# Logits of the next chunk computed in one run with the tap sums of this one, with the VectorE, GpSimd and SyncE work moved to suit

## The chip, the cores and the metric

One NeuronCore of one Trainium2 chip runs the whole kernel. The metric is device time in microseconds of one execution; lower is better. A kernel's figure is the median of its runs. The profile is one execution taken by the hardware profiler.

## The reference, cut to what matters

The input x is 2048 x 512 in bf16, layer-normalized to xn. Two branches start from xn: a local attention with 32 heads of 16, in which each position looks at 8 earlier ones at a distance of 2, and a gated feed-forward of width 1792.

```python
xn = layernorm(x)
q, k, v = split(xn @ wqkv)                      # 32 heads of 16
logits[s, w] = q[s] . k[s - 2 * w] / 4          # w = 0..7, positions below 0 masked
o[s] = sum_w softmax(logits)[s, w] * v[s - 2 * w]
s = o @ wo
g = silu((gelu(xn @ w_gate) * (xn @ w_up)) @ w_down)
out = x + s * g
```

## The kernel before

The positions are cut into four chunks of 512 (j = 0..3; the prediction calls them "tiles 0 to 3" where it speaks of the attention, and "tiles 8 to 11" are the blocks of 128 positions of chunk 2). For each chunk TensorE does a gate/up stage (14 pairs of projections), then q, k, v of the next chunk, then the down projection in four groups, with the output projection between them. The attention lies beside it: VectorE multiplies q by shifted k (`pk`), TensorE sums over the head with a matrix of ones that is only 32 columns wide (the logits), ScalarE takes exp, VectorE multiplies by shifted v (`pv`), and TensorE sums again (the tap sums and the denominators). These sums use a quarter of the array's columns each; four of them, writing to different partitions, run side by side (in the trace their starts lie 3 to 4 ns apart).

```python
def logits(j):                                  # 32 matmuls with 32 columns each
    nc.scalar.preload_act_table(AF.Exp)
    L = att.tile([P, NC, TQ], F32, name="L_ps", tag="quad")
    for wh in range(WH):
        for c in range(NC):
            for wl in range(WL):
                nc.tensor.matmul(L[H * wl : H * (wl + 1), wh, :], lhsT=dsum[:, c, :],
                                 rhs=st[j]["pk"][WL * wh + wl][:, c, :], ...)
    nc.scalar.activation(out=E[:], in_=L[:, 0:WH, :], func=AF.Exp, scale=SCALE)

# ... the places in the schedule, for j = 1..3
for w in range(W):
    at(("qkv", j, 9 + w) if w < 3 else ("down", j - 1, w // 3), qk_product, j, w)
at(("glu", j, 0), logits, j)                    # a run of 32-column matmuls
for i in range(8):
    at(("glu", j, 2 + i), av_product, j, i // 2, i % 2)
at(("glu", j, 11), denominators, j)             # a second run, with
at(("glu", j, 11), av_sums, j)                  # 8 + 32 such matmuls
```

`at(key, f, ...)` puts f into the program just ahead of the stage named by the key. All engines run their programs in order.

The softmax here doesn't subtract the row's maximum and nothing guards it: scores larger than these inputs give would overflow.

## Time and profile before

| | before |
|---|---|
| median of 6 runs | 229.99 us (229.64 to 230.21) |
| span of the profiled run | 228.0 us, granted clock 1.000 |
| TensorE busy | 222.4 us, 98% |
| VectorE, ScalarE busy | 147.6 us, 129.8 us |
| runs of 32-column matmuls | 8 |
| first logits matmul to start of the last matmul | 190.25 us |

The lines are in the prediction. In a trace, matmul records can be missing; then two neighbours seem 0.432 us apart and not 0.216. Weight loads are all recorded.

### The profile page before, as it was taken

The numbers are of one execution on the slowest core, as the hardware profiler recorded it, in microseconds if no ns is written. First come the engines' busy times: TensorE is split into PE (matmuls) and PEld (weight loads), VectorE is DVE, ScalarE is ACT, GpSimd is POOL, SyncE is SP. The second block draws the span as 40 slices with busy tenths as digits, with TensorE's granted clock in tenths as the row PEclk, the third lists the DMA queues.
The fourth block names the chain that finished last, engine by engine and source line by source line (L and its number), as shares of the span: only waits on it lengthen the run. The fifth ranks groups of instructions, "written<-read, shape, count | busy, mean of one in ns | idle before, by whom it ended". The sixth has DMA issues, their size and how long they took to land.

```text
span 228.0 us, 3495 instructions
## 1 busy us (share of the span) xinstructions
PE 222.4 (98%) x1300; PEld 106.8 (47%) x1320; DVE 147.6 (65%) x234; ACT 129.8 (57%) x213; POOL 12.8 (6%) x44
## 2 busy tenths in 40 slices
PE   8999999999999999999999999999999999999993
PEld 6864444444444444444444444444444444444453
DVE  4585996999496298865945369735476429943324
ACT  3779769774423876467621686746642387647210
POOL 1046023100000000110000000000000000000000
PEclk9999999999999999999999999999999999999999
DMA  6999589971399211110287511110149700001011
GB/s 166 354 372 372 146 169 197 247 202 38 101 195 206 70 25 29 26 29 0 92 169 168 139 30 23 26 35 5 39 119 206 169 27 3 0 6 26 0 45 48
DMA packets 31264, 24.62 MB, mean 108 GB/s; under 512 B 10896, under 2 KB 31248, under 8 KB 31248
## 3 DMA queue, kind: packets, MB, share of 16 engines
q1 hardware_dynamic: 31248, 24.41, 42.8%
q8 instruction: 10, 0.16, 0.3%
q14 instruction: 6, 0.05, 0.1%
HBM read 18.74 MB, written 4.34 MB: 101 GB/s over the span
## 4 chain that ended last, share of the span: by engine, by line
PE 95%; ACT 2%; issue 1%; DVE 0%; ACTq 0%; DVEq 0%
PE u_ps L238 21%; PE y_ps L394 21%; PE g_ps L238 19%; PE qkv_ps L238 17%; PE s_ps L410 6%; PE L_ps L295 3%; PE o_ps L357 3%; PE warm_ps L220 2%; PE q_ps L238 1%; ACT u L384 1%; ACT L382 1%; PE tr L203 1%; PE den_ps L315 0%; ACT xnT L212 0%; ACT ge L382 0%
## 5 line engine op out<-in xcount | busy, mean ns | idle before, releaser
L238 PE MATMUL u_ps<-xnT,wu_sb 128*128 128x512 bf16 x224 | 57.5, 379 | 0.3
L238 PE MATMUL g_ps<-xnT,wg_sb 128*128 128x512 bf16 x213 | 56.3, 379 | 0.4
L394 PE MATMUL y_ps<-wd_sb,h 128*128 128x512 bf16 (+1 forms) x236 | 50.2, 366 | 0.1
L386 DVE TENSOR_TENSOR h<-ge,u 128x512 bf16<-128x512 bf16 x56 | 23.7, 424 | 37.0 <-ACT u L384 36.6
L284 DVE TENSOR_TENSOR pk<-q_sb,k_sb 128x2048 bf16<-128x2048 bf16 x32 | 37.5, 1216 | 7.0 <-ACT k_sb L259 7.0
L382 ACT ACTIVATE ge<-g_ps 128x512 bf16<-128x512 f32 x56 | 33.5, 598 | 14.9 <-PE g_ps L238 13.8
L384 ACT ACTIVATE u<-u_ps 128x512 bf16<-128x512 f32 x56 | 33.5, 598 | 14.7 <-PE u_ps L238 14.7
L238 PE MATMUL qkv_ps<-xnT,wqkv_sb 128*128 128x512 bf16 (+1 forms) x203 | 40.5, 354 | 0.3
L343 DVE TENSOR_TENSOR pv<-E,v_arr 128x2048 bf16<-128x2048 bf16 x32 | 38.6, 1218 | 0.2 <-issue 0.2
L394 PEld LDWEIGHTS <-h 128*128 128x128 bf16 x238 | 23.3, 98 | 25.3
L238 PEld LDWEIGHTS <-wu_sb 128*128 128x128 bf16 x224 | 21.9, 98 | 26.6 <-issue 0.3
L238 PEld LDWEIGHTS <-wg_sb 128*128 128x128 bf16 x224 | 21.3, 98 | 27.3 <-issue 3.0
L402 ACT ACTIVATE sl<-y_ps 128x512 bf16<-128x512 f32 (+1 forms) x17 | 9.7, 572 | 41.4 <-PE y_ps L394 39.0
L238 PEld LDWEIGHTS <-wqkv_sb 128*128 128x128 bf16 x224 | 21.8, 98 | 19.8 <-issue 0.4
L418 DVE TENSOR_TENSOR m<-s_ps,sl 128x512 bf16<-128x512 f32 (+1 forms) x17 | 11.2, 657 | 22.2 <-PE s_ps L410 22.2
L410 PE MATMUL s_ps<-wo_sb,oT 128*128 128x512 bf16 (+1 forms) x66 | 15.8, 366 | 0.2
L262 ACT ACTIVATE vst<-qkv_ps 128x512 bf16<-128x512 f32 x16 | 9.6, 598 | 6.5 <-PE qkv_ps L238 6.5
L188 POOL TENSOR_TENSOR rstd<-rstd,mhalf 128x1 f32<-128x1 f32 x12 | 7.7, 640 | 87.4 <-DVE rstd L185 87.4
L259 ACT ACTIVATE k_sb<-qkv_ps 128x512 bf16<-128x512 f32 (+1 forms) x20 | 10.2, 516 | 3.5 <-PE qkv_ps L238 3.2
L369 DVE TENSOR_TENSOR oT<-o_ps,rb 128x1024 bf16<-128x1024 f32 x8 | 9.4, 1216 | 3.1 <-DMA rb<-rs_d 3.1
L256 ACT ACTIVATE q_sb<-qkv_ps 128x512 bf16<-128x512 f32 (+1 forms) x16 | 8.7, 544 | 3.2 <-PE qkv_ps L238 3.0
L410 PEld LDWEIGHTS <-oT 128*128 128x128 bf16 x68 | 6.7, 98 | 7.2
(46 smaller groups left out, 105.9 us busy)
## 6 DMA issues: line engine op xcount, KB each, us to landing
v_arr<-vT SPq DMA_DIRECT2D x16, 520.0 KB, 5.4
vT<-vst SPq DMA_DIRECT2D x16, 128.0 KB, 1.8
out_dram<-o_t SPq DMA_DIRECT2D x15, 128.0 KB, 1.8
wg_sb<-in_B_w_gate_dram SPq DMA_DIRECT2D x2, 896.0 KB, 10.7
wu_sb<-in_B_w_up_dram SPq DMA_DIRECT2D x2, 896.0 KB, 12.3
wd_sb<-in_B_w_down_dram SPq DMA_DIRECT2D x1, 1792.0 KB, 12.3
wqkv_sb<-in_A_wqkv_dram SPq DMA_DIRECT2D x3, 512.0 KB, 5.2
x_sb<-in_A_x_dram SPq DMA_DIRECT2D x3, 512.0 KB, 11.6
```

The lines of the kernel that those rows point to most:

```text
L238: nc.tensor.matmul(ps, lhsT=w[:, dk, lo : lo + P], rhs=xnT[j][:, dk, i0 : i0 + n], start=(dk == 0), stop=(dk == NC - 1),)
L259: nc.scalar.activation(out=k_sb[:, c, lo : lo + n], in_=ps, func=AF.Copy)
L262: nc.scalar.activation(out=vst[:], in_=ps, func=AF.Copy)
L284: nc.vector.tensor_tensor(out=pk[:], in0=st[j]["q"][:], in1=k_sb[:, :, off : off + TQ], op=ALU.mult)
L343: nc.vector.tensor_tensor(out=pv[:], in0=st[j]["E"][:, wh, :].unsqueeze(1).to_broadcast([P, 4, TQ]), in1=st[j]["va"][:, 4 * g : 4 * g + 4, ...
L382: nc.scalar.activation(out=ge[:], in_=g_ps[:], func=AF.Gelu_apprx_tanh)
L384: nc.scalar.activation(out=u[:], in_=u_ps[:], func=AF.Copy)
L386: nc.vector.tensor_tensor(out=h[:], in0=ge[:], in1=u[:], op=ALU.mult)
L394: nc.tensor.matmul(y[:], lhsT=st[j][fc][:, tt * P : (tt + 1) * P], rhs=wd_sb[:, fc, cols], start=(fc == 0), stop=(fc == NF - 1),)
L402: nc.scalar.activation(out=sl[:], in_=y[:], func=AF.Silu)
L410: nc.tensor.matmul(s[:], lhsT=st[j]["oT"][:, g, tt * P : (tt + 1) * P], rhs=wo_sb[:, g, cols], start=(g == 0), stop=(g == NC - 1),)
L418: nc.vector.tensor_tensor(out=m[:], in0=s[:], in1=sl[:], op=ALU.mult)
```

## The change

The intent is to enter and leave the 32-column form of the array less often: the logits of chunk j + 1 move into the same run as the denominators and tap sums of chunk j. Everything else serves that. The products for the logits are needed some 12 us earlier, so they are made in halves, and the q and k pieces of a chunk are projected in turns (two of q, two of k, and again) so that the first halves can start early; work of VectorE is moved out of their way; the v read of chunk 0 is moved forward; k gets a tile per chunk (two buffers in turn) and GpSimd copies the 16 columns of overlap; the last four products of chunks 1 to 3 (w = 4 to 7) share v's buffer, so v is read after the logits; the four output projections of a chunk come together at its end.

```diff
+    def sums(j):
+        if j + 1 < NJ:
+            nc.scalar.preload_act_table(AF.Exp)
+        denominators(j)
+        av_sums(j)
+        if j + 1 < NJ:
+            logits(j + 1)
+        reciprocals(j)
+        store_reciprocals(j)
+        spread_reciprocals(j)
+        if j + 1 < NJ:
+            load_v(j + 1)
 ... (for j = 1..3)
-        for w in range(W):
-            at(("qkv", j, 9 + w) if w < 3 else ("down", j - 1, w // 3), qk_product, j, w)
-        at(("glu", j, 0), logits, j)
+        at(("qkv", j, 2), k_halo, j)
+        for i in range(2):
+            at(("qkv", j, 4 + 4 * i), qk_products, j, range(W), 2 * i, 2)
 ... (normalization of chunk 2, from the gate/up stage to the down stage)
-        at(("glu", 0, 7 + i), moments, 2 * TPQ + i)
-        at(("glu", 0, 8 + i), normalize, 2 * TPQ + i)
+        at(("down", 0, 1), moments, 2 * TPQ + i)
+        at(("down", 0, 2), normalize, 2 * TPQ + i)
 ... (v of chunk 0)
-    at(("glu", 0, 0), transpose_by_dma, TPQ + 2)
+    at(("glu", 0, 0), transpose_by_dma, TPQ + 2, (0, 1))
     at(("glu", 0, 0), load_v, 0)
+    at(("glu", 0, 0), transpose_by_dma, TPQ + 2, (2, 3))
 ... (the down stage)
+            for tt in range(TPQ):
+                run("down", j, tt)
+                sl.append(down(j, tt, full))
+                if tt == 0:
+                    sums(j)
+            divide(j)
+            for tt in range(TPQ):
+                finish(j, tt, full, sl[tt])
 ... (longer programs)
+        for _ in range(20):
+            nc.gpsimd.memset(filler[:], 0.0)
+        n = 4 if j < 2 else 2        # pv of chunks 2 and 3 in halves
```

More of the change, by code (lines that the diff above doesn't have):

```diff
@@ L59 @@
     qp = pool("qp", 1)
-    ep = pool("ep", 2)
+    kp = pool("kp", 2)
+    ep = pool("ep", 1)
     vap = pool("vap", 1)
-    prod = pool("prod", 8)
-    hp = pool("hp", 16)
+    prod = pool("prod", 12)
+    hp = pool("hp", 14)
     xtp = pool("xtp", 2)
@@ L66 @@
     sm = pool("sm", 3)
+    slp = pool("slp", 4)
     sm2 = pool("sm2", 2)
@@ L141 @@
     dsum = const.tile([P, NC, H], BF16, name="dsum")
+    filler = const.tile([P, 1], F32, name="filler")
     def sum_constants():
+        for _ in range(20):
+            nc.gpsimd.memset(filler[:], 0.0)
         nc.gpsimd.memset(dsum[:], 0.0)
@@ L155 @@
     xnT = {}
-    k_sb = big.tile([P, NC, PAD + S], BF16, name="k_sb")
-    nc.vector.memset(k_sb[:, :, 0:PAD], 0.0)
+    k_sb = {0: kp.tile([P, NC, PAD + TQ], BF16, name="k_sb")}
+    nc.vector.memset(k_sb[0][:, :, 0:PAD], 0.0)
     stats = const.tile([P, NT, nc.vector.BN_STATS_DIM], F32, name="stats")
@@ L223, in warm_up, with transpose_by_dma @@
             )
-    def transpose_by_dma(t):
+    def transpose_by_dma(t, cs=range(NC)):
         j, i = divmod(t, TPQ)
-        if i == 0:
+        if i == 0 and 0 in cs:
             xnT[j] = xtp.tile([P, NC, TQ], BF16, name="xnT")
-        for c in range(NC):
+        for c in cs:
             nc.sync.dma_start(
@@ L257, in qkv @@
         elif which == 1:
-            lo = PAD + j * TQ + i0
-            nc.scalar.activation(out=k_sb[:, c, lo : lo + n], in_=ps, func=AF.Copy)
+            lo = PAD + i0
+            nc.scalar.activation(out=k_sb[j][:, c, lo : lo + n], in_=ps, func=AF.Copy)
         else:
@@ L268, in load_v @@
         if wls[0] == 0:
-            st[j]["va"] = vap.tile([P, DH, VW], BF16, name="v_arr")
+            st[j]["va"] = vap.tile([P, DH, VW], BF16, name="v_arr", tag="va")
         va = st[j]["va"]
@@ L279, in load_v, with k_halo, qk_products @@
             )
-    def qk_product(j, w):
-        pk = prod.tile([P, NC, TQ], BF16, name="pk", tag="prod")
-        off = PAD + j * TQ - w * DIL
-        nc.vector.tensor_tensor(
-            out=pk[:], in0=st[j]["q"][:], in1=k_sb[:, :, off : off + TQ], op=ALU.mult
-        )
-        st[j]["pk"][w] = pk
-    def logits(j):
-        nc.scalar.preload_act_table(AF.Exp)
-        L = att.tile([P, NC, TQ], F32, name="L_ps", tag="quad")
+    def k_halo(j):
+        k_sb[j] = kp.tile([P, NC, PAD + TQ], BF16, name="k_sb")
+        nc.gpsimd.tensor_copy(out=k_sb[j][:, :, 0:PAD], in_=k_sb[j - 1][:, :, TQ : TQ + PAD])
+    def qk_products(j, ws, c0, n):
+        for w in ws:
+            if w not in st[j]["pk"]:
+                if j and w >= WL:
+                    if w == WL:
+                        st[j]["pk4"] = vap.tile([P, WL, NC, TQ], BF16, name="pk4", tag="va")
+                    st[j]["pk"][w] = st[j]["pk4"][:, w - WL]
+                else:
+                    st[j]["pk"][w] = prod.tile([P, NC, TQ], BF16, name="pk", tag="prod")
+            off = PAD - w * DIL
+            nc.vector.tensor_tensor(
+                out=st[j]["pk"][w][:, c0 : c0 + n, :],
+                in0=st[j]["q"][:, c0 : c0 + n, :],
+                in1=k_sb[j][:, c0 : c0 + n, off : off + TQ],
+                op=ALU.mult,
+            )
+    def logits(j):
+        if j == 0:
+            nc.scalar.preload_act_table(AF.Exp)
+            quad = att.tile([P, NC, TQ], F32, name="L_ps", tag="quad")
+            L = [quad[:, wh, :] for wh in range(WH)]
+        else:
+            L = [mm.tile([P, TQ], F32, name="L_ps", tag="mm")[:] for _ in range(WH)]
+        E = st[j]["E"] = ep.tile([P, WH, TQ], BF16, name="E")
         for wh in range(WH):
@@ L295, in logits @@
                     nc.tensor.matmul(
-                        L[H * wl : H * (wl + 1), wh, :],
+                        L[wh][H * wl : H * (wl + 1), :],
                         lhsT=dsum[:, c, :],
@@ L301, in logits @@
                     )
-        E = st[j]["E"] = ep.tile([P, WH, TQ], BF16, name="E")
-        nc.scalar.activation(out=E[:], in_=L[:, 0:WH, :], func=AF.Exp, scale=SCALE)
+        for wh in range(WH):
+            nc.scalar.activation(out=E[:, wh, :], in_=L[wh], func=AF.Exp, scale=SCALE)
         if j == 0:
@@ L321, in denominators, with reciprocals @@
                 )
+        st[j]["den"] = den
+    def reciprocals(j):
+        den = st[j]["den"]
         rs = sm2.tile([P, P], BF16, name="rs")
@@ L342, in av_product @@
         lo = WL * DIL * (1 - wh)
-        nc.vector.tensor_tensor(
-            out=pv[:],
-            in0=st[j]["E"][:, wh, :].unsqueeze(1).to_broadcast([P, 4, TQ]),
-            in1=st[j]["va"][:, 4 * g : 4 * g + 4, lo : lo + TQ],
-            op=ALU.mult,
-        )
+        n = 4 if j < 2 else 2
+        for d in range(0, 4, n):
+            nc.vector.tensor_tensor(
+                out=pv[:, d : d + n, :],
+                in0=st[j]["E"][:, wh, :].unsqueeze(1).to_broadcast([P, n, TQ]),
+                in1=st[j]["va"][:, 4 * g + d : 4 * g + d + n, lo : lo + TQ],
+                op=ALU.mult,
+            )
         st[j]["pv"][g, wh] = pv
@@ L400, in down @@
             )
-        sl = sm.tile([P, n], BF16, name="sl")
+        sl = slp.tile([P, n], BF16, name="sl")
         nc.scalar.activation(out=sl[:], in_=y[:], func=AF.Silu)
@@ L434 @@
         at(("qkv", 0, i), normalize, TPQ + i)
-        at(("glu", 0, 7 + i), moments, 2 * TPQ + i)
+        at(("down", 0, 1), moments, 2 * TPQ + i)
         if i < 2:
             at(("glu", 0, i), transpose, TPQ + i)
-        at(("glu", 0, 8 + i), normalize, 2 * TPQ + i)
+        at(("down", 0, 2), normalize, 2 * TPQ + i)
         at(("glu", 1, 0), transpose_by_dma, 2 * TPQ + i)
         at(("glu", 1, 10 + i), moments, 3 * TPQ + i)
-        at(("qkv", 2, 2 * i), normalize, 3 * TPQ + i)
+        at(("qkv", 2, i), normalize, 3 * TPQ + i)
@@ L442 @@
         at(("glu", 2, 0), transpose_by_dma, 3 * TPQ + i)
     for w in range(W):
-        at(("glu", 0, w), qk_product, 0, w)
+        at(("glu", 0, w), qk_products, 0, [w], 0, NC)
     at(("glu", 0, 9), logits, 0)
     for i in range(8):
-        at(("glu", 0, 11 + i) if i < 3 else ("qkv", 1, (0, 1, 2, 4, 5)[i - 3]),
-           av_product, 0, i // 2, i % 2)
-    at(("qkv", 1, 8), denominators, 0)
-    at(("qkv", 1, 8), av_sums, 0)
-    at(("qkv", 1, 8), store_reciprocals, 0)
-    at(("qkv", 1, 10), spread_reciprocals, 0)
@@ L454 @@
-    at(("down", 0, 0), divide, 0)
-    for j in range(1, NJ):
-        for w in range(W):
-            at(("qkv", j, 9 + w) if w < 3 else ("down", j - 1, w // 3), qk_product, j, w)
-        for i in range(TPQ):
-            at(("down", j - 1, i), load_v, j, [i])
-        at(("glu", j, 0), logits, j)
-        for i in range(8):
-            at(("glu", j, 2 + i), av_product, j, i // 2, i % 2)
-        at(("glu", j, 11), denominators, j)
-        at(("glu", j, 11), av_sums, j)
-        at(("glu", j, 11), store_reciprocals, j)
-        at(("glu", j, 11), spread_reciprocals, j)
-        at(("qkv", j + 1, 6) if j + 1 < NJ else ("down", j, 0), divide, j)
+        at(("glu", 0, 11 + i) if i < 3 else ("qkv", 1, 0), av_product, 0, i // 2, i % 2)
@@ new lines, in sums @@
+    def sums(j):
+        if j + 1 < NJ:
+            nc.scalar.preload_act_table(AF.Exp)
+        denominators(j)
[7 more added lines that the diff above has]
+            load_v(j + 1)
+    for j in range(1, NJ):
+        at(("qkv", j, 2), k_halo, j)
+        for i in range(2):
+            at(("qkv", j, 4 + 4 * i), qk_products, j, range(W), 2 * i, 2)
+        for i in range(8):
+            at(("glu", j, 3 + i), av_product, j, i // 2, i % 2)
@@ L471 @@
+    at(("glu", NJ - 1, 12), sums, NJ - 1)
     HT = TPQ // 2
@@ L517 @@
         if j + 1 < NJ:
-            for i in range(12):
+            for i, fo in enumerate((0, 1, 4, 5, 2, 3, 6, 7, 8, 9, 10, 11)):
                 run("qkv", j + 1, i)
-                qkv(j + 1, i)
-        todo = []
-        for tt in range(TPQ):
-            run("down", j, tt)
-            last = j * TPQ + tt == NT - 1
-            for cols in (slice(0, D // 2), slice(D // 2, D)) if last else (slice(0, D),):
-                sl = down(j, tt, cols)
-                if todo:
-                    finish(*todo.pop())
-                if last:
-                    finish(j, tt, cols, sl)
-                else:
-                    todo.append((j, tt, cols, sl))
-        if todo:
-            finish(*todo.pop())
+                qkv(j + 1, fo)
+            full = slice(0, D)
+            sl = []
+            for tt in range(TPQ):
[6 more added lines that the diff above has]
+                finish(j, tt, full, sl[tt])
+        else:
+            full, half = slice(0, D), (slice(0, D // 2), slice(D // 2, D))
+            sl = [down(j, tt, full) for tt in range(TPQ - 1)]
+            divide(j)
+            finish(j, 0, full, sl[0])
+            finish(j, 1, full, sl[1])
+            sl3 = down(j, 3, half[0])
+            finish(j, 2, full, sl[2])
+            finish(j, 3, half[0], sl3)
+            sl3 = down(j, 3, half[1])
+            finish(j, 3, half[1], sl3)
 _INS = ['A_x', 'A_wqkv', 'A_wo', 'B_x', 'B_w_gate', 'B_w_up', 'B_w_down']
```

## The prediction

> **What bounds the kernel now.** I read the page first: the busy line, the clock row and the chain that ended last.
>
> ```profile
> PE 222.4 (98%) x1300; PEld 106.8 (47%) x1320; DVE 147.6 (65%) x234; ACT 129.8 (57%) x213; POOL 12.8 (6%) x44
> ...
> PEclk9999999999999999999999999999999999999999
> ...
> PE 95%; ACT 2%; issue 1%; DVE 0%; ACTq 0%; DVEq 0%
> ```
>
> TensorE is busy nearly the whole span, its clock is never taken down, and the chain is TensorE. But busy is not peak, so I compared starts. Between two full 512-column matmuls in a stream the starts lie 0.2158 us apart (four in 0.86 us in the chain). With that step the whole program adds up: gate and up 448 x 0.2158 = 96.7; q, k, v 160 x 0.2158 + 64 x 0.109 = 41.5; down 210 x 0.2158 + 28 x 0.109 = 48.4; output projection 60 x 0.2158 + 8 x 0.109 = 13.8; logits and tap sums, four column tiles at once, 64 steps = 13.8; denominators 32 matmuls, 8 steps of 0.056 = 0.45; warm-up, transposes and their wait until q starts at 6.88 us: 6.0 from 0.84 us; later transposes about 1. That is 221.7 us. The span of 228.0 holds besides 0.84 before the first matmul and 3.4 after the last (products, sum and the store). So only 228.0 - 221.7 - 4.2 = 2.1 us are lost inside TensorE's stream, and nothing in the middle can win more than that. The waits view agrees: hardly a TensorE wait has another engine's name. (Steps of 0.432 us in the trace are all but one a missing matmul record, 20 of 1320.)
>
> Where the 2.1 us lie I read from the chain in order of time and from TensorE's timeline (columns: start, duration, what):
>
> ```profile
> 92.73 0.86 PE u_ps L238 x4
> 93.60 0.23 PE den_ps L315 x8
> 93.82 1.73 PE o_ps L357 x32
> 95.55 0.32 PE g_ps L238
> ```
>
> ```profile
> 92.57 1.03 PE L238 MATMUL u_ps<-xnT,wu_sb 128*128 128x512 bf16 x4
> 93.53 0.29 PE L315 MATMUL den_ps<-E,hsum 128*32 128x128 bf16 x8
> 93.65 1.90 PE L357 MATMUL o_ps<-pv,hsum 128*32 128x512 bf16 x32
> 95.48 1.04 PE L238 MATMUL g_ps<-xnT,wg_sb 128*128 128x512 bf16 x3
> ```
>
> The four u matmuls should let go at 92.57 + 4 x 0.216 = 93.43, but the first 32-column matmul starts at 93.53: 0.09 us to enter the run. The tap sums should let go at 93.65 + 8 x 0.216 = 95.38, and the next full matmul starts at 95.48: 0.10 us to leave. With some 0.01 at the first step inside, a run of 32-column matmuls costs 0.21 us over its own work. I took all eight runs of the kernel (four of logits, four of denominators with tap sums): each 0.209 to 0.210 us, 1.68 us in all. It is most of the 2.1; one stall of 0.21 near 20.4 us, behind a table load of ScalarE, is the rest.
>
> **What the Trainium skill says.** TensorEngine Tiling (Array Packing), Key Properties: "Changing tiling mode (not just tile) drains the TensorE". The trace agrees, 0.21 us per visit; the page gives no figure. TensorE: Matmul & The Clock Gate, Back-to-back issue gap: N / 2.4 + 2.5 ns for a lone gap, that is 215.8 for 512; here 215.8 also in the stream, so that page's 131 ns for a sustained stream is not seen. VectorE: DVE Perf Modes, the TRN2 errata: a large tile pays the fixed cost once, small tiles pay it each. The trace agrees: in a row 128x2048 products lie 1.135 apart, and h of 128x512 takes 0.34 of the engine, so a fixed 0.07 beside 1.067 and 0.267. ScalarE: Activation LUTs, What ACT_TABLE_LOAD costs: about 1283 ns and a drain; the trace has 1283 for each load, and no long drain after it.
>
> **The change part by part.**
>
> (1) Joint runs. Logits of tile j+1 move from the start of its gate/up stage into the run of denominators and tap sums of tile j, now after the first down matmul group. Runs of 32-column matmuls: 8 become 5 (logits 0; three joint; sums of tile 3). Gain 3 x 0.21 = 0.63 us on TensorE, straight on the path. Matmul counts do not change, and tail and head are the same, so this is the whole certain gain.
>
> (2) The products for the next logits must now be ready earlier; this is the danger. Tile 1 is tightest. Before, VectorE runs without a pause:
>
> ```profile
> 42.44 1.22 DVE L343 TENSOR_TENSOR pv<-E,v_arr 128x2048 bf16<-128x2048 bf16 x1
> ...
> 46.85 5.76 DVE L343 TENSOR_TENSOR pv<-E,v_arr 128x2048 bf16<-128x2048 bf16 x5
> 52.53 0.95 DVE L324 RECIPROCAL rs<-den_ps 128x128 bf16<-128x128 f32 x1
> ```
>
> Moments and normalization of tiles 8 to 11 leave the first gate/up stage, so the first pv can start after the h before it, about 40.95; with h11 to h13 between (each when ScalarE's copy is done) the last five pv start at 45.8 and VectorE is free at 45.8 + 5 x 1.135 = 51.5. The 16 half products of 128x1024 then take about 0.60 each (0.533 + 0.07; eight whole ones would be 0.55 less in all): ready at 61.1. TensorE: qkv of tile 1 from 44.70, 48 x 0.2158 = 10.36, down 14 x 0.2158 = 3.02, entry 0.09, denominators 0.12, sums 1.73: logits from 60.0; the group that needs the last product is its seventh, at 60.0 + 6 x 0.216 = 61.3. Product ready 61.1 to 61.3 with the signal, needed 61.3: a tie, wait 0 to 0.8, I count 0.1. For tiles 2 and 3 (no pv left over) there are some 3 us to spare.
>
> Reading v of chunk 0 before the last two transposes of tile 6 brings its issue forward by about 2.7 us; in the kernel before it landed up to 12.0 us after an issue from 27.98 on, about 40, so for a pv at 40.95 it is needed; it is not a gain by itself.
>
> (3) Reciprocals and the division. Tile 0: reciprocal until 62.2, then store, spread and landing as before (53.51 to about 59, 5.3 us): 67.5; moments 4 x 1.0 and normalization 4 x 0.33 lie in that time; division 2.36 until 69.9. The first output projection comes at 61.85 + 9.06 (three down groups) = 70.9. One us spare, more in later tiles. Hidden.
>
> (4) The four output projections are now together at the end. VectorE takes 1.07 per tile (m, then o_t) against TensorE's 0.86, so the last store is issued some 2.5 us after the next gate/up stage begins, and SyncE issues the 16 transposes behind it:
>
> ```profile
> 73.08 1.40 SPq L421 DMA_DIRECT2D out_dram<-o_t  x2
> 74.58 21.68 SPq L230 DMA_TRANSPOSE xnT<-xn  x16
> 96.65 0.33 SPq L328 DMA_DIRECT2D rs_d<-rs  x1
> ```
>
> Before, they started 0.15 after the stage (74.43) and qkv began 26.4 after it. Now: start +2.5, last one starts +22.5, lands (2.4) about +24.9; qkv begins at 14 x 1.726 = +24.2 and wants the last piece at its fourth matmul, +24.8. Another tie, for tiles 2 and 3; I count 0.05 each.
>
> (5) Split pv of tiles 2 and 3: 8 more VectorE instructions each, about 0.07 x 8 = 0.5 us in a stage where VectorE has 15.4 of 26.4. One Silu/Exp pair more per joint run: one more table load of 1.28 in a stage where ScalarE has 5.6 of 17.3. Twenty memsets of GpSimd, about 0.1 each, push dsum from 20.3 to at most 22.4; it is read at 34. The halo copies are small. All hidden. v now has 2.08 MB to read in one go after the logits: about 12 us (chunk 0), issued near 66, so 78, against pv near 80.5.
>
> Sum: -0.63 + 0.1 + 0.1 = -0.4; I take 229.84 - 0.5 = 229.3, as the schedule looks trimmed to these ties.
>
> **Rivals.** (a) Products late: VectorE becomes the bound between qkv and logits of tile 1, 0.8 us and all gain gone, 229.9; for it speaks the tie, against it the moved moments. (b) Transposes late at tiles 2 and 3, up to 0.5 each: 230.2. For it speaks that SyncE issues in order, against it that only the fourth matmul needs the last piece. (c) A late v read or instruction fetches on the longer programs, 1 us or more: 230.5 to 232; nothing in the trace before shows such a fetch on the path. (d) A gain over 2% (4.6 us) has no source: only 2.1 us are lost.
>
> **Range and chances.** All ties won gives 229.2, with the spread of the runs before (229.64 to 230.21) down to 228.8; both lost gives about 230.3. So 228.8 to 230.3, faster 0.01, same 0.97, slower 0.02.
>
> **What would show it.** Five runs of 32-column matmuls with 0.21 each; logits of tile 1 with no gap before their seventh step; no gap at the fourth matmul of qkv in tiles 2 and 3; division done before the first output projection. The prediction is wrong if TensorE shows a new gap over 1 us, or if a joint run costs much more than 0.21.

## The result and the profile after

| | before | after |
|---|---|---|
| median of 6 runs each | 229.99 us | 229.37 us (228.95 to 229.64) |
| ratio | | 0.9972, 95% interval 0.9959 to 0.9986 |
| span of the profiled run | 228.0 us | 227.6 us |
| runs of 32-column matmuls | 8 | 5 |
| first logits matmul to last matmul | 190.25 us | 189.65 us |

A ratio here is the mean time of one kernel's runs over the mean of the other's runs of the same rounds, so it is not quite the ratio of the two medians. The verdict is "same" at the 2% mark; the interval lies below 1, so the gain of 0.6 us is there.

The page of the changed kernel, the lines that answer to those of before:

```profile
PE 223.2 (98%) x1320; PEld 107.4 (47%) x1320; DVE 150.4 (66%) x274; ACT 135.0 (59%) x220; POOL 18.1 (8%) x67
...
PEclk9999999999999999999999999999999999999999
...
PE 97%; ACT 1%; DVE 0%; issue 0%; DVEq 0%
```

TensorE is still the chain. Its busy time is not comparable: all 1320 matmuls are recorded this time, and 1300 were before. The chain in order of time (start, duration, what), around the first two joint runs:

```profile
58.33 0.23 PE den_ps L343 x8
58.55 1.73 PE o_ps L391 x32
60.28 1.78 PE L_ps L323 x32
62.06 9.17 PE y_ps L428 x42
...
114.19 1.73 PE L_ps L323 x32
115.92 9.17 PE y_ps L428 x42
```

Logits now follow the tap sums without a way out and in between. The 42 down matmuls of 0.2158 us are 9.06 us by themselves; the 0.11 more is the way out of the run, paid once. In the first joint run the logits take 1.78 us and in the second 1.73: the 0.05 is a wait for the last product of chunk 1. By start times the four other runs cost 0.21 us each over their own work, as before, and the first joint run 0.26.

VectorE's timeline in the changed kernel:

```profile
41.26 1.23 DVE L377 TENSOR_TENSOR pv<-E,v_arr 128x2048 bf16<-128x2048 bf16 x1
...
46.02 5.76 DVE L377 TENSOR_TENSOR pv<-E,v_arr 128x2048 bf16<-128x2048 bf16 x5
51.70 9.72 DVE L305 TENSOR_TENSOR pk<-q_sb,k_sb 128x1024 bf16<-128x1024 bf16 x16
61.34 0.95 DVE L356 RECIPROCAL rs<-den_ps 128x128 bf16<-128x128 f32 x1
```

The products of chunk 1 are done near 61.4, which is the moment at which the logits need the last of them. The queue of SyncE, and TensorE's weight loads at the start of q, k, v of chunk 2:

```profile
73.38 3.52 SPq L455 DMA_DIRECT2D out_dram<-o_t  x4
76.94 21.21 SPq L237 DMA_TRANSPOSE xnT<-xn  x16
```

```profile
99.33 1.19 PEld L245 LDWEIGHTS <-wqkv_sb 128*128 128x128 bf16 x7 [0.32 <-DMA xnT<-xn]
```

The transposes start 2.4 us into the gate/up stage, and the fourth weight load of q stands 0.32 us for the last of them (it landed at 99.28). Weight loads run ahead of the matmuls, here by 0.21 us, so in this run no matmul waited.

### The profile page after: what moved, and what is told of

Its sections match the earlier page's. It is cut to its first block, busy times and chain, and to the rows that moved or that the text cites. A ratio compares the mean times of both kernels' runs of the same rounds, so it can differ in the third digit from the quotient of the medians.

```text
span 227.6 us, 3610 instructions
## 1 busy us (share of the span) xinstructions
PE 223.2 (98%) x1320; PEld 107.4 (47%) x1320; DVE 150.4 (66%) x274; ACT 135.0 (59%) x220; POOL 18.1 (8%) x67
## 4 chain that ended last, share of the span: by engine, by line
PE 97%; ACT 1%; DVE 0%; issue 0%; DVEq 0%
PE y_ps L428 21%; PE u_ps L245 21%; PE g_ps L245 21%; PE qkv_ps L245 17%; PE s_ps L444 6%; PE L_ps L323 3%; PE o_ps L391 3%; PE warm_ps L227 2%; PE q_ps L245 1%; PE tr L210 1%; ACT L416 1%; PE den_ps L343 0%; ACT xnT L219 0%; ACT ge L416 0%; ACT vst L269 0%; DVE m L452 0%
## 5 line engine op out<-in xcount | busy, mean ns | idle before, releaser
L245 PE MATMUL g_ps<-xnT,wg_sb 128*128 128x512 bf16 x224 | 57.5, 379 | 0.0
L305 DVE TENSOR_TENSOR pk<-q_sb,k_sb 128x1024 bf16<-128x1024 bf16 (+1 forms) x56 | 39.0, 761 | 4.6 <-ACT k_sb L266 4.6
L377 DVE TENSOR_TENSOR pv<-E,v_arr 128x1024 bf16<-128x1024 bf16 (+1 forms) x48 | 39.7, 862 | 0.0
L444 PE MATMUL s_ps<-wo_sb,oT 128*128 128x512 bf16 (+1 forms) x68 | 14.8, 367 | 0.0
```

The lines of the kernel that those rows point to most:

```text
L245: nc.tensor.matmul(ps, lhsT=w[:, dk, lo : lo + P], rhs=xnT[j][:, dk, i0 : i0 + n], start=(dk == 0), stop=(dk == NC - 1),)
L305: nc.vector.tensor_tensor(out=st[j]["pk"][w][:, c0 : c0 + n, :], in0=st[j]["q"][:, c0 : c0 + n, :], in1=k_sb[j][:, c0 : c0 + n, off : off ...
L377: nc.vector.tensor_tensor(out=pv[:, d : d + n, :], in0=st[j]["E"][:, wh, :].unsqueeze(1).to_broadcast([P, n, TQ]), in1=st[j]["va"][:, 4 * ...
L444: nc.tensor.matmul(s[:], lhsT=st[j]["oT"][:, g, tt * P : (tt + 1) * P], rhs=wo_sb[:, g, cols], start=(g == 0), stop=(g == NC - 1),)
```

## The experiments

All are edits of the changed kernel and gave correct results. First logits matmul to last matmul is called the body; it is 190.25 us before and 189.65 us after. Times are medians of 5 or 6 runs.

### The changed kernel again, twice

No edit; it was run with each of two sets of experiments.

> The changed kernel once more, as the yardstick for the other runs of this chip. Theory: 0.6 us under the kernel before (about 0.9974 of it): three runs of 32-column matmuls fewer at 0.21 us, less 0.05 us of waiting for the products of tile 1. Rival (a gain by chance of the first comparison): no difference.

> The changed kernel again, the yardstick of this chip. Expected 0.997 of the kernel before, 229.3 us.

Measured: 229.28 us against 230.13, ratio 0.9961 (0.9948 to 0.9974), and later 229.56 against 229.89, ratio 0.9983 (0.9966 to 1.0001). Three comparisons with the kernel before give 0.9972, 0.9961 and 0.9983, so 0.9972 is a fair middle and a single comparison carries about 0.3 us of uncertainty. The bodies were 189.94 and 189.90: in both profiles TensorE did wait for the last transpose of chunk 2, 0.29 and 0.24 us, which it had not in the first profile of this kernel. In all three the transposes start 2.4 us into the stage; from the first issue to the third it took 3.8 us in the repeats and 3.5 us in the first profile. The tie of step 4 goes either way from run to run.

### Logits in a run of their own

```diff
-        if j + 1 < NJ:
-            logits(j + 1)                # in sums(j), behind av_sums(j)
+                if tt == 1:              # one down group later
+                    nc.scalar.preload_act_table(AF.Exp)
+                    logits(j + 1)
+                    load_v(j + 1)
```

> Joint runs undone and all else kept: the logits of the next tile come one down group after the tap sums, as a run of their own, so there are 8 runs of 32-column matmuls again. Theory: 3 x 0.21 - 0.05 = 0.58 us slower than the changed kernel, so level with the kernel before (ratio 1.000, within 0.001), with 8 runs of 0.21 us in the trace. Rival (the gain comes from the moved VectorE and DMA work): it stays with the changed kernel, 0.997.

Measured: 229.86 us against 229.28 for the changed kernel on the same chip, 0.58 us slower; ratio to before 0.9988 (0.9973 to 1.0004). The body is 190.41. Its chain:

```profile
58.20 1.73 PE o_ps L391 x32
59.93 2.05 PE y_ps L428 x9
61.98 0.05 issue
62.03 1.03 PE y_ps L428 x4
63.06 1.84 PE L_ps L323 x32
64.90 2.27 PE y_ps L428 x10
```

The logits again take 1.84 us, as in the kernel before, 0.11 of it at the way in, and all eight runs have their 0.21. The rest of the change is still in this kernel and buys nothing that shows: the interval to the kernel before includes 1. The gain is the joint run. (The body is 0.76 over that of the changed kernel's first profile: 0.66 - 0.05 for the runs, with 0.22 for each as the next experiment shows, and 0.14 for a transpose that came late.)

### Four times as many runs

```diff
+                between = {2: lambda: av_sums(j, [1]), 4: lambda: av_sums(j, [2]),
+                           6: lambda: sums_end(j)} if tt == 1 else None
+                sl.append(down(j, tt, full, between))
```

The tap sums of chunks 0 to 2 are cut in four, and pairs of full matmuls of the second down group stand between the quarters; `sums_end` is the last quarter and the logits.

> The suspected cost multiplied: the tap sums of tiles 0 to 2 are cut into four runs, with full matmuls of the second down group between them; 9 visits more than the changed kernel, 14 in all, the same matmuls otherwise. Theory: 9 x 0.21 = 1.89 us slower than the changed kernel, 1.3 us slower than the kernel before (ratio about 1.0055). Rival (a visit costs nothing by itself, the 0.21 us are how the records are modelled): within 0.3 us of the changed kernel.

Measured: 230.87 us, 1.59 us slower than the changed kernel on the same chip; ratios to before 1.0035 and 0.9961, so 1.7 us by the ratios. Against the kernel before it is 0.74 us slower and not 1.3, since in these rounds the changed kernel itself came out 0.85 us faster than that kernel. The body is 191.71, 2.06 more than 189.65 (1.77 more than 189.94, the changed kernel's body in these rounds). The chain shows the two ways apart:

```profile
58.08 0.43 PE o_ps L393 x8
58.51 0.54 PE y_ps L431 x2
59.05 0.55 PE o_ps L393 x8
59.59 0.54 PE y_ps L431 x2
```

Two full matmuls are 0.43 us and eight of 32 columns are 0.43 us. Each group takes 0.11 or 0.12 longer when the form of the array changes ahead of it. A visit costs a little more than I had counted: by starts, the first full matmul after a run takes 0.226 us to the next one and not 0.216, so it is 0.21 + 0.01 = 0.22. Nine more visits at 0.22 are 1.98; less the 0.05 wait, which is gone, plus 0.13 for a late transpose, that is the 2.06. So the cost of a visit is real time, and nine visits cost nine times as much as one.

### Moments back in the gate/up stage

```diff
-        at(("down", 0, 1), moments, 2 * TPQ + i)
-        at(("down", 0, 2), normalize, 2 * TPQ + i)
+        at(("glu", 0, 7 + i), moments, 2 * TPQ + i)
+        at(("glu", 0, 8 + i), normalize, 2 * TPQ + i)
```

> Moments and normalization of tiles 8 to 11 go back to the first gate/up stage, as in the kernel before; joint runs kept. Theory: the first tap product starts near 42.4 us instead of 41.3, the products of tile 1 are ready about 0.85 us later, and since they were already 0.05 us late TensorE waits 0.8 to 0.9 us inside the first joint run: 0.85 us slower than the changed kernel (ratio to before about 1.001), the run's surplus 1.1 us instead of 0.26. Rival (VectorE has room there and the move was worth nothing): no difference to the changed kernel.

Measured: 230.59 us, 1.31 us slower than the changed kernel on the same chip; ratio to before 1.0018 (1.0003 to 1.0033), slower than the kernel before. The body is 190.79, and the surplus of the first joint run is 1.40 us in place of 0.26. Its chain there is no longer TensorE:

```profile
53.87 9.04 DVE pk L305 x15
62.91 0.04 issue
62.95 0.59 PE L_ps L323 x5
```

So the moved VectorE work is what keeps the joint run's gain. I had put it at 0.85 us; the body says 1.14. It was too low because I took the difference of the absolute times at which the last five pv start (46.85 in the kernel before, 46.02 in the changed one), and the head of the second profile was 0.25 us longer; from the first logits matmul on, the difference is 1.08.

### One more transpose in the queue

```diff
+        if i == 2:                       # written again, long landed
+            at(("glu", 1, 0), transpose_by_dma, 2 * TPQ, [1])
+            at(("glu", 2, 0), transpose_by_dma, 3 * TPQ, [1])
```

> SyncE issues one more DMA transpose in front of the last ones of tiles 2 and 3 (a piece that has long landed is written again, the result is unchanged): 1.27 us more in its queue in each. Theory (the tie of my step 4: the last piece lands within 0.1 us of its need in tile 2, some 0.25 us early in tile 3): TensorE waits 1.2 us at the fourth matmul of qkv in tile 2 and 1.0 in tile 3, 2.2 us slower than the changed kernel, ratio to before about 1.0065. Rival (transposes have room): no difference to the changed kernel, 0.997.

Measured: 231.68 us against 229.98 before, ratio 1.0076 (1.0056 to 1.0096). TensorE's weight loads in chunk 2:

```profile
98.70 0.53 PEld L245 LDWEIGHTS <-wqkv_sb 128*128 128x128 bf16 x3
100.89 1.19 PEld L245 LDWEIGHTS <-wqkv_sb 128*128 128x128 bf16 x7 [1.66 <-DMA xnT<-xn]
```

The matmuls of chunk 2 waited 1.33 us and those of chunk 3 0.96 us: one queue entry of 1.27 us costs TensorE its whole length in chunk 2, where there was no room, and three quarters of it in chunk 3. The rest of the body's 192.48 (2.83 over 189.65) was not in the expectation: the last quarter of v of chunk 0 landed at 41.74 us in this profile and not at 41.18, the first pv started at 41.82, and the first joint run waited 0.56 us for its products. The edit lies far behind that read, so I take it for chance (not shown); it is an example of a late read of v that delays the products of chunk 1.

### v behind all transposes of block 6

```diff
-    at(("glu", 0, 0), transpose_by_dma, TPQ + 2, (0, 1))
+    at(("glu", 0, 0), transpose_by_dma, TPQ + 2)
     at(("glu", 0, 0), load_v, 0)
-    at(("glu", 0, 0), transpose_by_dma, TPQ + 2, (2, 3))
```

> The read of v of chunk 0 goes back behind all four transposes of tile 6. In the changed kernel its last quarter lands at 41.18 us and the first tap product starts at 41.26. Theory: it lands near 42.1 again, the first tap product starts 0.9 us later, the products of tile 1 are ready some 0.55 us later, and TensorE waits that much more inside the first joint run: 0.55 us slower than the changed kernel, level with before. Rival (a transfer that is hidden anyway): no difference to the changed kernel.

Measured: 229.32 us, ratio 0.9974 (0.9961 to 0.9987), and a body of 189.65, that of the changed kernel. My theory fell. SyncE's queue and the first pv of this run:

```profile
20.68 5.47 SPq L237 DMA_TRANSPOSE xnT<-xn  x4
26.33 2.73 SPq L279 DMA_DIRECT2D v_arr<-vT  x4
```

```profile
41.31 1.22 DVE L377 TENSOR_TENSOR pv<-E,v_arr 128x2048 bf16<-128x2048 bf16 x1 [0.26 <-DMA v_arr<-vT]
```

The same part of SyncE's queue in the changed kernel:

```profile
20.56 2.83 SPq L237 DMA_TRANSPOSE xnT<-xn  x2
26.45 2.70 SPq L279 DMA_DIRECT2D v_arr<-vT  x4
```

The read is issued at 26.33 here and at 26.45 in the changed kernel, although there it has two transposes fewer ahead of it. It cannot go out before the last store of v has landed. In the changed kernel that is at 26.33, and the read follows 0.12 us later (0.12 in its two repeats as well); the queue has stood still from 23.4 on. Here the store landed at 26.02, the four transposes held the queue until 26.15, and the read followed 0.31 us after the store. So the order was worth some 0.2 us of the read; the rest of the two transposes was hidden in the wait for the store. And these 0.2 us had room: the first tap product waited for v here, yet the last five started 11.7 us after the first logits matmul in both kernels.

### Gelu table loaded early

```diff
+    nc.scalar.preload_act_table(AF.Gelu_apprx_tanh)
     for i in range(NC):                  # v of chunk 0
```

> One table load of ScalarE is moved ahead of the v copies of chunk 0, so the first gelu does not wait for it. Theory: the only other gap in TensorE's stream, 0.21 us near 20.6 us, goes: 0.2 us faster than the changed kernel (ratio to before about 0.9962), provided that the later copies do not make a new wait. Rival: the copies of v come 0.8 us late and TensorE waits for a PSUM buffer there instead, no gain.

Measured: 229.13 us against 229.98, ratio 0.9968 (0.9955 to 0.9982); against the run above, from the same rounds, 0.19 us less by the medians and 0.14 by the ratios, which is within their noise. The trace is clearer: the gap of 0.21 us at 20.6 is gone, but the wait in the first joint run grew from 0.05 to 0.17, because TensorE came 0.21 earlier and VectorE, held by the read of v, did not. Half of the gain was turned into that wait.

### Whole products

```diff
-        for i in range(2):
-            at(("qkv", j, 4 + 4 * i), qk_products, j, range(W), 2 * i, 2)
+        at(("qkv", j, 8), qk_products, j, range(W), 0, NC)
```

> The products for the next logits as 8 whole ones once all of k is there, in place of 16 halves of which the first 8 start after two of four pieces. VectorE saves 0.55 us per tile. Theory: they can only start near 52.7 us in tile 1 (106.6 in tile 2) and end 9.1 later, and every step of the second half of the logits needs the last one: TensorE waits about 0.9 us in each of the three joint runs, 2.6 us slower than the changed kernel in all, ratio to before about 1.008. Rival (fewer, larger VectorE instructions win): 0.3 us faster than the changed kernel.

Measured: 231.36 us, ratio 1.0061 (1.0049 to 1.0074), body 192.07. The chain at the first joint run:

```profile
53.49 8.05 DVE pk L305 x7
61.53 0.04 issue
61.58 1.02 PE L_ps L323 x13
```

TensorE waited 0.77, 0.80 and 0.76 us in the three joint runs, 2.3 together. Fewer and larger instructions saved VectorE time and lost TensorE time: what counts is when the first half can start.

### Short programs

The 20 filler memsets are taken out and the tap products of chunks 2 and 3 are whole.

```diff
-        for _ in range(20):
-            nc.gpsimd.memset(filler[:], 0.0)
-        n = 4 if j < 2 else 2
+        n = 4
```

> The parts of the change that only lengthen the programs of GpSimd and VectorE are undone: no filler memsets, the tap products of tiles 2 and 3 whole again. Theory: both lie where their engines have room (the sum constants are ready at 23.3 us in the changed kernel and read at 34), so no change, within 0.2 us of the changed kernel. Rival (they move an instruction fetch off the path): 0.5 us or more slower, with a gap on an engine that the trace puts down to issue.

Measured: 229.71 us, ratio to before 0.9996 (0.9981 to 1.0011); the changed kernel in the same rounds 229.56, ratio 0.9983 (0.9966 to 1.0001). The intervals overlap. The trace has a body of 189.65, equal to that of the changed kernel's first profile, the same waits, and no new gap that is put down to issue. What these parts are for is not settled: in the trace they cost and give nothing.

### A version without the waits

```diff
+    nc.scalar.preload_act_table(AF.Gelu_apprx_tanh)
-                if tt == 0:
+                if tt == (1 if j == 0 else 0):
                     sums(j)
-        at(("down", 0, 1), moments, 2 * TPQ + i)
-        at(("down", 0, 2), normalize, 2 * TPQ + i)
+        at(("down", 0, 2), moments, 2 * TPQ + i)
+        at(("down", 0, 3), normalize, 2 * TPQ + i)
```

> A better version: the early table load, and the first joint run one down group later (with the moments and normalization of tiles 8 to 11 one group later too), so that the products of tile 1 have 3 us more. Theory: the gap of 0.21 us at 20.6 us goes and the wait inside the first joint run (0.05 to 0.26 us in the runs so far) goes too: 0.25 to 0.45 us faster than the changed kernel, ratio to before about 0.9957, all five runs of 32-column matmuls with 0.21. Rival: the reciprocals of tile 0 come 3 us later, the division is late and TensorE waits before the first output projection instead.

Then the same with the transposes issued right behind `divide(j)`, ahead of the output stores:

```diff
-        at(("glu", 1, 0), transpose_by_dma, 2 * TPQ + i)
-        at(("glu", 2, 0), transpose_by_dma, 3 * TPQ + i)
+        at(("xnT", 0, 0), transpose_by_dma, 2 * TPQ + i)
+        at(("xnT", 1, 0), transpose_by_dma, 3 * TPQ + i)
             divide(j)
+            run("xnT", j, 0)
```

> The same with the 16 transposes of tiles 2 and 3 issued in front of the four output stores, not behind them. Theory: the last piece lands 8 us before its need, so the wait of 0.07 to 0.14 us at the fourth qkv matmul of tile 2 cannot occur: 0 to 0.1 us faster than the run without it. Rival: the stores behind the transposes hold their buffers up and VectorE or TensorE waits later.

Measured: 228.90 us, ratio to before 0.9961 (0.9949 to 0.9974), and 228.99 us, 0.9959 (0.9947 to 0.9972); the changed kernel in the same rounds 229.56. Both are faster than the changed kernel by some 0.6 us of medians there; by the ratios 0.5. That yardstick was the slowest of the changed kernel's three; against the middle ratio of 0.9972 they gain 0.25 to 0.3 us, the size expected. The chain of the second at its first joint run:

```profile
61.39 1.73 PE o_ps L391 x32
63.12 1.73 PE L_ps L323 x32
64.84 5.29 PE y_ps L428 x24
```

The logits take 1.73 us: no wait. All five runs cost 0.21 in both. The first of the two has the gap at the transposes (0.24 us in chunk 2) and a body of 189.85; in the second it is gone and the body is 189.60, the lowest of all. Their times do not tell the two apart, the traces do. The second is the version I would keep.

## Why the prediction was right, point by point

- **TensorE is the bound and only 2.1 us are to be had.** Right. The best version won only from the gaps that I listed (eight visits of 0.21, one stall of 0.21): three visits, which took the body from 190.25 to 189.60, and the stall of 0.21 ahead of it. No experiment found another source.
- **Step 1, three visits fewer, 0.63 us.** Right. Body 190.25 to 189.65; undone it comes back (0.58 us), multiplied it grows (9 visits, 1.89 predicted, 2.06 in the body with 0.08 of other waits in it, which makes 0.22 a visit). What the array does in that time was not shown. The prediction took the drain, of which the page that it cites speaks, as confirmed by the 0.21 us; the trace shows the cost and not its cause. An obvious rival is that at a border the weight load no longer runs ahead: it starts with the first matmul, and takes 0.09 to 0.10 us, the size of each side. Against it speaks a load in q of chunk 2 of the changed kernel, which came only 0.015 us before its matmul, without a change of form, and left the step at 0.216. No run made for the purpose decides between the two.
- **Step 2, the tie at the products of chunk 1.** Right in kind and size: I counted 0.1, it was 0.05 in the first profile and 0.05 to 0.56 in the others. Undoing the moved moments made it 1.19. The need was put 0.16 us too late: 44.70 is the chain's time, and by start times the first q matmul of chunk 1 is at 44.54.
- **Step 2, the read of v comes 2.7 us earlier by the new order.** This was wrong. It came 1.5 us earlier between the two profiles (27.98 to 26.45). Of that 1.0 is the last store of v, which landed at 26.33 and not at 27.33 (why is open), and some 0.5 the order: the read followed the store by 0.65 us before and by 0.12 after. The landing was misread too. The 12.0 us in the kernel before are those of the last quarter from its own issue at 30.01, so v landed at 42.06 there and not at about 40. That v is needed at 41 was right: it landed at 41.18 and was used at 41.26.
- **Step 3, the division is hidden.** Right: the reciprocals ended at 62.3, the division started at 67.46 (67.5 predicted), and the first output projection came at 71.07.
- **Step 4, the tie at the transposes.** Right in kind, but the wait was counted too small: nothing in the first profile, 0.24 to 0.29 in chunk 2 in the two repeats, 0.05 counted per chunk. In chunk 3 there was no wait in the changed kernel.
- **Step 5, hidden work.** Right in effect. Two sizes were off: the 20 memsets took 3.30 us and not 2.1, so the constants for the logits were ready at 23.3 us, and v of chunk 1 landed at 80.17 and not at 78, by the misread 12.0 us (its four quarters took 14.5 us from the first issue). That left 0.76 us to the first tap product at 80.93. Neither reached TensorE.

The sum and the figure don't quite match: the terms add up to -0.43, the prediction took 0.5, and took it from 229.84, the single profiled run, where the median is 229.99. From the median the terms give 229.56, and measured were 229.37. So the mechanism and the range were right, and that the figure of 229.3 came within 0.1 us is in part luck.

## What to carry to other kernels

When one engine's stream is full, add up its own steps from start times and see what is left over; here it was 2.1 us of 228, and that number alone ruled out a gain over 2%. A change that wins tenths of a microsecond by reordering lives on the slack of everything that it moves, so write down for each moved piece when it will be ready and when it is needed, and mark the ties. When a queue seems to be ordered badly, look first at what its next entry waits for: a new order ahead of a wait is worth only what reaches beyond that wait, here some 0.2 to 0.5 us in place of 2.7.

## What the Trainium skill lacked or had wrong

- TensorEngine Tiling (Array Packing), Key Properties, says that changing the mode drains the array but gives no cost. Here one visit to 128x32 tiles from full matmuls cost 0.21 us in every run without another wait: 0.093 in, 0.106 out, 0.01 at the first step inside; with the 0.01 at the first full step behind it, 0.22. Going from one set of sums to the next inside the form cost nothing.
- TensorE: Matmul & The Clock Gate, Back-to-back issue gap, has 131 ns per matmul for a sustained stream of N = 512 with weight loads. Here such streams, 42 matmuls long, keep 215.8 ns, which is that page's value for an isolated matmul. The page disagrees with itself: other sections of it have 215.7 ns from start to start for back-to-back matmuls, as measured here.
- ScalarE: Activation LUTs, What ACT_TABLE_LOAD costs, adds a drain of about 1380 ns to the load. In the changed kernel a load ran from 19.32 to 20.60 us, the copy before it ended at 19.30 and the next gelu started at 20.61; no such drain is seen on either side.
- No page that I read says how much the head of a kernel varies: the first q matmul started between 6.56 and 7.72 us in these profiles (in the latest of them TensorE waited for a load of weights), more than the whole gain looked for. That this makes the spread of the timed runs is likely and was not shown; the profiled run with the latest start is also the slowest of its six (230.26 us).
